# Value tiles with rows of 80 elements in place of 65 in a block-sparse attention and gated-MLP kernel

## The chip, the core and the metric

The kernel runs on one core of one Trainium2 chip. The metric is the device time of one execution in microseconds (us). The engines are TensorE (PE for its matrix products, PEld for its weight loads), VectorE (DVE), ScalarE (ACT), GpSimd (POOL) and the DMA queues, here nearly all issued by SyncE (SP).

## What is computed

Four batches of eight heads, 768 positions, 64 features for each head. A block-sparse mask (blocks of 32: neighbours, first and last, and three sampled blocks for each row of blocks) is applied to the scores; the softmax of them weights the value rows. The heads' outputs, side by side, are the input of a gated MLP whose second half is normalized and mixed over positions.

```python
scores = np.where(mask, scale * (q @ k.T), -1e9)
attn = exp(scores - max) / sum
x = (attn @ v) for each head, heads side by side      # 768 x 512 per batch
h = relu(x @ w_in); u, v = h[..., :512], h[..., 512:]
v_s = w_spatial @ ((v - mean) / sqrt(var + 1e-6)) + b_spatial
out = (u * v_s) @ w_out
```

## The kernel before

The 768 positions of a head are six chunks of 128 (NCH = 6). Heads are taken in pairs; there are 16 pairs (NP), four to a batch. For each head the kernel forms transposed scores chunk by chunk (keys on the partitions, queries along the row; L415 and L428), takes their exponential on ACT into `a_all` (L420 and L431), and multiplies with the values (L458 and L476). Masking rides in the score product as extra rows of `kq`.

**The value tiles.** There are six buffers `vv0` to `vv5` (line 85), used in turn by the pairs. Each holds, on each partition, 2 heads x 6 chunks x VA elements of bf16, with VA = 65: 64 features and a 1.0 written once at the start by POOL (L171). With the ones column the attention product also gives the softmax's denominator. A row of 65 elements has 130 bytes, and the rows lie one behind the other, so row (h, ci) begins 780 h + 130 ci bytes behind the tile's start. A tile takes 1,560 bytes of a partition, and the tiles start 1,568 bytes apart, each on a multiple of 32 bytes. Values are loaded as fp32 (`st_v`) and cast into `vv` by POOL (the helper `cast`, L137).

**The attention products.** One product takes a 128x128 block of `a_all` as the weights and one row of `vv` (128 partitions x 65) as the moving operand, and accumulates six chunks into 65 columns of a PSUM tile `ps_av`. The first batch, pairs 0 to 3, is worked in units, and `av_unit` (L458) issues eight products at a time, 36 times, 288 in all. The other twelve pairs go through `av_full` (L476), which issues the six products of one block of queries, 144 times, 864 in all. I call such a row of six or eight products a run.

**The order of the work** is written out by hand as slots. A slot issues the score products of one block, one run of attention products from some slots earlier, and, dealt out evenly, steps of the MLP of the batch before (L561, L630), so that PE has other matrix products between the runs. Scores go through two PSUM buffers (`sc`), so PE may be at most two slots ahead of ACT. After the last slot (178 us) only the last batch's MLP is left. Nothing in the order depends on the shape of `vv`.

Of the kernel before, what the change touches and what calls it, by code (L numbers as in the profile page):

```python
# [11 lines left out]
BF16 = mybir.dt.bfloat16  # L12
# [14 lines left out]
def kernel(  # L27
# [22 lines left out]
    NCH = S // 128  # L50
# [9 lines left out]
    VA = D + 1  # L60
# [9 lines left out]
    const = ctx.enter_context(tc.tile_pool(name="const", bufs=1))  # L70
# [11 lines left out]

    kq = const.tile([128, H, 2 * S], BF16, name="kq")
    NVV = 6
    vv = [const.tile([128, 2, NCH, VA], BF16, name=f"vv{s}") for s in range(NVV)]
    MR = slice(D, KR)
    MX = slice(D, 128)
    K_, Q_ = slice(0, S), slice(S, 2 * S)
# [344 lines left out]
    def av_tile(key, n):  # L433
        ps = psum.tile([128, 512], FP32, tag="av", bufs=2, name="ps_av")
        av_ref[key] = ps[:, 0:n * VA].rearrange("p (c d) -> p c d", d=VA)
        x_ref[key] = ps[:, 512 - TW // 2:512].bitcast(BF16)

    def normalize(ps, out, n):
        rc = work.tile([128, NCH, 1], FP32, tag="rc", bufs=2)
        nc.vector.reciprocal(out=rc[:, 0:n], in_=ps[:, :, D:VA])  # L440
        nc.vector.tensor_tensor(out=out, in0=ps[:, :, 0:D],  # L441
                                in1=rc[:, 0:n].to_broadcast([128, n, D]), op=ALU.mult)

    def av_unit(u, e):
        t, p = UNITS[u]
        if e == 0:
            av_tile(u, 2 * TC)
        for i in range(8 * e, 8 * e + 8):
            g, ci = divmod(i, NCH)
            if t == "h":  # L450
                h, qc, to, n = p, g, g, 2 * TC
                pp = 0
            else:
                (h, qc), n, pp = divmod(g, TC), TC, p
                to = qc * 2 + h
            at = (h * NCH + ci) * n * 128 if t != "h" else ci * n * 128
            at += qc * 128
            nc.tensor.matmul(out=av_ref[u][:, to, :], lhsT=a_ref[u][:, at:at + 128],  # L458
                             rhs=vv[pp % NVV][:, h, ci, :],
                             start=(ci == 0), stop=(ci == NCH - 1))  # L460
        if e == 2:
            a_ref.pop(u)
            if t == "h":
                if p == 0:
                    xn_ref[0] = work.tile([128, 2 * TC, 2, D], BF16, tag="xn0", bufs=1, name="xn0")
                normalize(av_ref.pop(u), xn_ref[0][:, :, p, :], 2 * TC)
            else:
                xn_ref[u] = work.tile([128, TC, 2, D], BF16, tag="xn3", bufs=3, name="xn3")
                normalize(av_ref.pop(u), xn_ref[u].rearrange("p c h d -> p (c h) d"), 2 * TC)

    def av_full(j, qc):
        p, h = divmod(j, 2)
        if qc == 0:
            av_tile(j, NCH)
        for ci in range(NCH):
            nc.tensor.matmul(out=av_ref[j][:, qc, :],  # L476
                             lhsT=a_ref["h", j][:, ci, qc * 128:(qc + 1) * 128],
                             rhs=vv[p % NVV][:, h, ci, :],
                             start=(ci == 0), stop=(ci == NCH - 1))
        if qc == NCH - 1:  # L480
            a_ref.pop(("h", j))
            if h == 0:
                xn_ref["p", p] = work.tile([128, NCH, 2, D], BF16, tag="xn", bufs=2, name="xn")
            normalize(av_ref.pop(j), xn_ref["p", p][:, :, h, :], NCH)
# [361 lines left out]
    for s in range(NS + LAG + 2):  # L846
        if s < S0:
            qk_unit(*divmod(s, 3))
        elif s < NS:
            j, ci = divmod(s - S0, NCH)  # L850
            qk_full(j + H, ci)
        early = at.get(s, [])
        for f in pre.get(s, []):
            f()
        for u, e in av_at.get(s, []):
            av_unit(u, e)
        if 0 <= s - LAG - S0 and s - LAG < NS:
            j, qc = divmod(s - LAG - S0, NCH)
            av_full(j + H, qc)
        for f in early:  # L860
            f()
        run_queue()
        for f in late.get(s, []):
            f()
        while post:
            post.pop(0)()
# [31 lines left out]
```

## Time and profile before

| | |
|---|---|
| three runs | 209.82, 210.37, 211.2 us; median 210.37 us |
| profiled execution, first to last instruction | span 208.3 us |
| PE busy | 201.0 us (97%), 2203 products recorded |
| ACT busy | 168.4 us (81%) |
| DVE busy | 146.8 us (70%) |
| POOL busy | 89.4 us (43%) |

The page gives the profiled execution by its span; the median run is 2.1 us longer than that span, and what lies around the span is taken to be these 2.1 us. Busy time of PE is the union of the products' durations; products overlap (one of 65 columns lasts 194 ns and the next starts long before it ends), so a full PE row doesn't say how fast PE goes. What a product costs in a stream is the time from its start to the next one's start, which the chain of waits shows.

### The profile page before, as it was taken

The numbers are of one execution on the slowest core, as the hardware profiler recorded it, in microseconds if no ns is written. First come the engines' busy times: TensorE is split into PE (matmuls) and PEld (weight loads), VectorE is DVE, ScalarE is ACT, GpSimd is POOL, SyncE is SP. The second block draws the span as 40 slices with busy tenths as digits, with TensorE's granted clock in tenths as the row PEclk, the third lists the DMA queues.
The fourth block names the chain that finished last, engine by engine and source line by source line (L and its number), as shares of the span: only waits on it lengthen the run. The fifth ranks groups of instructions, "written<-read, shape, count | busy, mean of one in ns | idle before, by whom it ended". The sixth has DMA issues, their size and how long they took to land.

```text
span 208.3 us, 5489 instructions
## 1 busy us (share of the span) xinstructions
PE 201.0 (97%) x2203; PEld 138.0 (66%) x2225; DVE 146.8 (70%) x315; ACT 168.4 (81%) x222; POOL 89.4 (43%) x186
## 2 busy tenths in 40 slices
PE   6899999999999999999999999999999999999993
PEld 6599888777766776667556676667665567445551
DVE  6888776989876766575975585456875666576871
ACT  6899999999999999989899878889899884266021
POOL 6888989767927964006757600006210000013000
PEclk9999999999999999999999999999999999999999
DMA  5999899999999999499987920499402010610016
GB/s 143 338 362 357 275 383 270 206 247 389 253 253 308 259 300 208 139 199 386 292 176 206 139 41 0 164 189 335 75 0 41 0 37 4 250 57 0 0 70 232
DMA packets 53053, 39.48 MB, mean 190 GB/s; under 512 B 33956, under 2 KB 47652, under 8 KB 53028
## 3 DMA queue, kind: packets, MB, share of 16 engines
q1 hardware_dynamic: 52596, 38.74, 70.0%
q10 hardware_dynamic: 432, 0.39, 0.6%
q8 instruction: 17, 0.28, 0.5%
q14 instruction: 8, 0.07, 0.1%
HBM read 24.77 MB, written 6.29 MB: 149 GB/s over the span
## 4 chain that ended last, share of the span: by engine, by line
PE 87%; DVE 4%; ACT 4%; DMA 2%; issue 1%; POOL 0%; ACTq 0%
PE ps L428 21%; PE ps_moe L630 17%; PE ps_moe L561 13%; PE ps_av L476 12%; PE ps L415 7%; PE ps_av L458 4%; PE ps_t L561 4%; PE ps_t L630 4%; PE ps_sc L630 2%; ACT a_all L420 2%; DVE stats L594 2%; DVE vn L185 2%; DMA st_q<-in_q_dram 2%; PE ps_sc L561 1%; PE ps L263 1%
## 5 line engine op out<-in xcount | busy, mean ns | idle before, releaser
L431 ACT ACTIVATE a_all<-ps 128x768 bf16<-128x768 f32 x144 | 113.4, 812 | 13.8 <-PE ps L428 6.2
L428 PE MATMUL ps<-kq 128*128 128x512 bf16 (+1 forms) x288 | 70.3, 326 | 0.3
L476 PEld LDWEIGHTS <-a_all 128*128 128x128 bf16 x864 | 46.6, 98 | 19.0
L476 PE MATMUL ps_av<-vv,a_all 128*128 128x65 bf16 x864 | 51.1, 194 | 0.1
L428 PEld LDWEIGHTS <-kq 128*128 128x128 bf16 x288 | 27.9, 97 | 23.6
L137 POOL CAST nat<-st_k 128x256 bf16<-128x256 f32 (+3 forms) x37 | 17.7, 509 | 38.7 <-DMA st_k<-in_k_dram 38.7
L420 ACT ACTIVATE a_all<-ps 128x1024 bf16<-128x1024 f32 x35 | 33.5, 1027 | 0.3
L630 PE MATMUL ps_moe<-w_spt,vn 128*128 128x512 bf16 (+1 forms) x144 | 33.1, 325 | 0.0
L598 POOL TENSOR_SCALAR std<-mv 128x3 f32<-128x3 f32 (+1 forms) x9 | 3.4, 376 | 48.7 <-DVE mv L595 48.5
L661 DVE TENSOR_TENSOR sb<-ps_moe,b_row 128x512 f32<-128x512 f32 x18 | 12.4, 690 | 14.5 <-PE ps_moe L630 14.2
L630 PE MATMUL ps_moe<-xt,w_in_t 128*128 128x256 bf16 (+1 forms) x108 | 21.7, 299 | 0.2
L415 PE MATMUL ps<-kq 128*128 128x256 bf16 x135 | 20.8, 275 | 0.8 <-DVE kq L211 0.6
L561 PE MATMUL ps_moe<-w_in_t,xt 128*128 128x512 bf16 x65 | 20.2, 378 | 0.2
L137 POOL CAST vv<-st_v 128x256 bf16<-128x256 f32 (+2 forms) x37 | 18.5, 533 | 3.9 <-DMA st_v<-in_v_dram 3.8
L137 POOL CAST nat<-st_q 128x256 bf16<-128x256 f32 (+2 forms) x41 | 19.2, 496 | 1.6 <-DMA st_q<-in_q_dram 1.5
L561 PE MATMUL ps_moe<-w_out_t,un 128*128 128x512 bf16 x64 | 19.4, 378 | 0.2
L441 DVE TENSOR_TENSOR xn<-ps_av,rc 128x384 bf16<-128x384 f32 (+1 forms) x36 | 18.5, 513 | 1.4 <-DVE rc L440 0.2
L664 DVE TENSOR_TENSOR un<-sb,un 128x512 bf16<-128x512 f32 x24 | 17.4, 727 | 1.5
L630 PEld LDWEIGHTS <-vn 128*128 128x128 bf16 x192 | 15.5, 97 | 4.4
L594 DVE BATCH_NORM_STATS2 stats<-vn 128x6 f32<-128x512 bf16 x24 | 16.5, 688 | 1.5 <-ACT vn L589 0.9
L211 DVE COPY osb<-ps_moe 128x512 f32<-128x512 f32 x12 | 8.3, 689 | 11.2 <-PE ps_moe L561 9.3
L211 DVE COPY kq<-tt 64x1536 bf16<-64x1536 bf16 x24 | 15.4, 641 | 0.6 <-DMA tt<-nat 0.2
(94 smaller groups left out, 241.6 us busy)
## 6 DMA issues: line engine op xcount, KB each, us to landing
out_dram<-osb SPq DMA_DIRECT2D x23, 256.0 KB, 2.1
st_k<-in_k_dram SPq DMA_DIRECT2D x15, 384.0 KB, 4.6
st_v<-in_v_dram SPq DMA_DIRECT2D x15, 384.0 KB, 6.2
st_q<-in_q_dram SPq DMA_DIRECT2D x12, 384.0 KB, 4.9
ws_f<-in_moe_w_spatial_dram SPq DMA_DIRECT2D x6, 384.0 KB, 5.5
w_f<-in_moe_w_in_dram SPq DMA_DIRECT2D x8, 256.0 KB, 6.3
w_f<-in_moe_w_out_dram SPq DMA_DIRECT2D x4, 256.0 KB, 5.4
st_q<-in_q_dram SPq DMA_DIRECT2D x3, 256.0 KB, 6.9
```

Of the source, the lines that this page charges most:

```text
L137: eng.tensor_copy(out=dst, in_=src)
L211: nc.vector.tensor_copy(out=o, in_=i)
L415: nc.tensor.matmul(out=ps[:, at:at + n * TW], lhsT=kq[:, h, ci * 128:(ci + 1) * 128], rhs=kq[:, h, qcols(t0, n)], start=True, stop=True)
L420: nc.scalar.activation(out=out, in_=ps, func=AF.Exp, scale=0.125)
L428: nc.tensor.matmul(out=ps[:, n0:n1], lhsT=kq[:, j % H, ci * 128:(ci + 1) * 128], rhs=kq[:, j % H, S + n0:S + n1], start=True, stop=True)
L431: nc.scalar.activation(out=a_ref["h", j][:, ci, :], in_=ps[:, 0:S], func=AF.Exp, scale=0.125)
L441: nc.vector.tensor_tensor(out=out, in0=ps[:, :, 0:D], in1=rc[:, 0:n].to_broadcast([128, n, D]), op=ALU.mult)
L476: nc.tensor.matmul(out=av_ref[j][:, qc, :], lhsT=a_ref["h", j][:, ci, qc * 128:(qc + 1) * 128], rhs=vv[p % NVV][:, h, ci, :], start=(ci == ...
L561: nc.tensor.matmul(out=ref["ps"][:, 0:w], lhsT=lhs(i), rhs=rhs(i), start=(i == 0), stop=(i == n - 1))
L594: nc.vector.bn_stats(out=stats, in_=self.vn[:, tcc, :])
L630: nc.tensor.matmul(out=o.rearrange("p (c t) -> p c t", c=n), lhsT=lhs(i)[:, (d0 + x) * 128:(d0 + x + 1) * 128], rhs=rhs(i), start=(i == 0) ...
L664: nc.vector.tensor_tensor(out=self.in_place(*area), in0=sb, in1=self.in_place(*area), op=ALU.mult)
```

## The change

The rows of a value tile become 80 elements (160 bytes) long, and the products read the first 65 of them. Row (h, ci) then begins 960 h + 160 ci bytes behind the tile's start, and the tiles are 1,920 bytes apart. Everything that is allocated behind the six tiles lies 2,112 bytes further on. The casts and the memset of the ones write the same elements at the new step. The instructions of every engine and their order are the same as before.

```diff
     NVV = 6
-    vv = [const.tile([128, 2, NCH, VA], BF16, name=f"vv{s}") for s in range(NVV)]
+    VS = 80
+    vv = [const.tile([128, 2, NCH, VS], BF16, name=f"vv{s}") for s in range(NVV)]
...
             nc.tensor.matmul(out=av_ref[u][:, to, :], lhsT=a_ref[u][:, at:at + 128],
-                             rhs=vv[pp % NVV][:, h, ci, :],
+                             rhs=vv[pp % NVV][:, h, ci, 0:VA],
                              start=(ci == 0), stop=(ci == NCH - 1))
...
                              lhsT=a_ref["h", j][:, ci, qc * 128:(qc + 1) * 128],
-                             rhs=vv[p % NVV][:, h, ci, :],
+                             rhs=vv[p % NVV][:, h, ci, 0:VA],
                              start=(ci == 0), stop=(ci == NCH - 1))
```

## Prediction

> **What bounds the kernel now.** I read the cores first, then who waits, then stretches of the span, then the chain. One core, full clock; and PE, once started, hardly waits for anyone:
>
> ```profile
> core 0: 208.3 us, clock 1.000
> PE wps L179 <- DVE tiny L157: 1.0, 1, 1.0
> PE psq L276 <- POOL nat L137: 0.6, 1, 0.6
> PE ps L415 <- DVE kq L211: 0.6, 1, 0.6
> ```
>
> These three are all of PE's own waits (us in total, times, longest). The stretches, with each engine's busy time:
>
> ```profile
> 11.00:43.00 32.00, 31.83 (x495) 28.01 (x498) 25.67 (x65) 31.52 (x34) 27.40 (x44) 1.00 1.07 309
> 43.00:178.00 135.00, 134.20 (x1484) 89.13 (x1497) 93.59 (x182) 117.88 (x158) 51.02 (x111) 1.00 0.72 177
> 178.00:208.00 30.00, 26.50 (x151) 14.31 (x150) 19.00 (x39) 10.23 (x18) 2.30 (x4) 1.00 0.26 97
> ```
>
> After the stretch's length the columns are PE, PEld, DVE, ACT, POOL. From 43 to 178 us PE is full and ACT has 17 of 135 us free: PE sets the pace there. From 11 to 43 us (the first batch, L458) PE and ACT are both full, ACT with 32.00 - 31.52 = 0.48 us free. So a nanosecond taken off a product's step comes off the time in the second stretch, and only within ACT's 0.48 us in the first.
>
> **What one attention product costs.** The chain of waits gives streams of products with no wait in them (start, length, then engine, tile, line, count):
>
> ```profile
> 14.64 0.45 PE ps L263 x8
> 183.88 1.73 PE ps_t L561 x8
> 187.34 0.87 PE ps_t L630 x8
> 11.60 0.51 PE ps_av L458 x16
> 49.53 0.19 PE ps_av L476 x6
> ```
>
> The first three are products of 128, 512 and 256 columns, each with its own weight load: 0.45/8 = 56 ns, 1.73/8 = 216 ns and 0.87/8 = 109 ns. Per column that is (216 - 56)/384 = 0.417 ns. Down from 128 columns to 65 it leaves 56.3 - 63 x 0.417 = 30.0 ns, down from 256 it leaves 108.8 - 191 x 0.417 = 29.1 ns; with 10 ns of rounding on each piece the two agree between 29.4 and 29.8. I take 29.6 ns as the step of a 65-column product that nothing disturbs. The attention products take 0.51/16 = 31.9 ns (L458) and 0.19/6 = 32 ns (L476). The finer number for L476 comes from its group:
>
> ```profile
> L476 PE MATMUL ps_av<-vv,a_all 128*128 128x65 bf16 x864 | 51.1, 194 | 0.1
> L458 PE MATMUL ps_av<-vv,a_all 128*128 128x65 bf16 x288 | 14.7, 194 | 0.0
> L476 PEld LDWEIGHTS <-a_all 128*128 128x128 bf16 x864 | 46.6, 98 | 19.0
> ```
>
> 51.1 us over 144 runs is 354.9 ns a run; less one duration of 194 ns, five steps remain: 32.2 ns each. So each attention product is 32.2 - 29.6 = 2.6 ns slower than its columns ask. Is the row's place the cause? The trace holds a test. In head 0 the rows of a run begin 0, 2, 4, 6, 8, 10 bytes past a multiple of 16; in head 1 they begin 12, 14, 0, 2, 4, 6 past one. A row that doesn't begin on a multiple of 16 shares its first 16 bytes with the end of the row that was read just before, unless it is the first of its run. So a run of head 0 has five rows that share and a run of head 1 has four. L476 alone, the twelve stretches with head 0 (first, last, sum) and the twelve with head 1:
>
> ```profile
> 46.20:50.68 4.48, 2.13 (x36) 1.00 1.03 354
> ...
> 168.86:173.91 5.05, 2.13 (x36) 1.00 0.21 42
> sum 59.56, PE 25.57; mean PE 2.13
> ```
>
> ```profile
> 51.03:55.52 4.49, 2.12 (x36) 1.00 1.21 253
> ...
> 174.15:178.08 3.93, 2.12 (x36) 1.00 0.18 67
> sum 60.77, PE 25.48; mean PE 2.12
> ```
>
> Each sum holds 72 runs of six. Head 1 is (25.57 - 25.48)/72 = 1.25 ns shorter a run, with one sharing row fewer. The place of a row does count, and an aligned row is the quicker one.
>
> **The change, part by part.**
>
> *The reads.* All twelve rows of a tile now begin on a multiple of 32 bytes, and none shares its first 16 bytes with the row before. The lower end is to let each sharing row that goes give what the one in head 1 gives: 4.5 rows a run x 1.25 ns x 144 runs = 0.81 us, and about 5.5 rows x 1.25 ns x 36 runs = 0.25 us in L458: 1.06 us. The upper end is that all 1,152 products fall to the lowest step above, 29.4 ns: 864 x 2.8 + 288 x 2.5 = 3.1 us. I take a point near the upper end, because in today's runs every aligned row is followed by a sharing one, which may wait for what the aligned row did not; a single replacement then shows only part, while after the change no such follower is left. With the undisturbed step of 29.6 ns: L476 gives 864 x 2.6 ns = 2.25 us, all of it in the stretch where PE alone sets the pace. L458 gives 288 x (31.9 - 29.6) = 0.66 us, of which ACT's free 0.48 us lets 0.48 us through. Sum: 2.25 + 0.48 = 2.73 us.
>
> *A rule that speaks against this.* The Trainium skill's page "SBUF — State Buffer" (Specifications (TRN2)) gives SBUF 16-byte lines, says that a line needs at least two hits for full bandwidth and that each crossing to a new line costs. A row of 130 bytes touches nine such lines at any even start, so by counting lines nothing changes; and the new layout leaves one lone element in the ninth line of every row, which by the two-hits rule is a cost that before only rows on a multiple of 16 had. The two sums above disagree with that second half: head 1, which has more such rows, is the quicker. No row here separates the crossing cost itself.
>
> *The writes.* POOL casts the same elements with a step of 160 bytes in place of 130:
>
> ```profile
> L137 POOL CAST vv<-st_v 128x256 bf16<-128x256 f32 x30 | 12.7, 460 | 2.7 <-DMA st_v<-in_v_dram 2.6
> L137 POOL CAST nat<-st_k 128x256 bf16<-128x256 f32 x30 | 12.8, 464 | 38.4 <-DMA st_k<-in_k_dram 38.4
> L171 POOL MEMSET vv<- 128x12 bf16 x6 | 0.4, 180 | 0.0
> ```
>
> Into `nat`, whose rows of 64 lie on multiples of 128 bytes, the same cast takes 464 ns against 460 into today's rows, so alignment is worth between -4 and +4 ns a cast; over 30 casts that is 0.1 us of POOL time either way, and PE's list has no wait for `vv` at all. I take 0. What hides it is POOL's free time (51 of 135 us busy). The six memsets write 12 lone elements, each in a place of its own before and after: 0, with at most their 0.4 us either way on a POOL queue that runs ahead of the first casts.
>
> *The shift* of the later tiles by 2,112 bytes keeps their places to a multiple of 64 bytes. No row shows such a shift; between the heads above, a different place inside a tile moved a run by 1.25 of 355 ns, and that for rows that changed against 16 bytes, so I bound it at 0.4% of PE's time on other lines, 0.5 us either way, and take 0.
>
> **The sum.** The profiled span of 208.3 us less 2.73 us is 205.6 us; with the 2.1 us that lie between the span and the median run, 207.6 us, or 1.3% under 210.37.
>
> **The rivals.**
>
> *Part only.* The aligned row's gain really is 1.25 ns and doesn't grow when its neighbours are aligned too, or the weight loads (98 ns each, six of them overlapping in a run) hold the pair of load and product near 31 ns. For it: the only measured replacement gave that little. Against: streams of other widths with the same loads stand on the straight line of columns. Time: 210.4 - 1.1 = 209.3 us.
>
> *No effect: the change doesn't do what it says.* The step of 32.2 ns is set by the weight load or by the odd number of columns, and the heads differ for another reason (their place in the slots). For it: loads and products come in pairs in every run. Against: 0.09 us between the heads over 72 runs, in sums that differ in the same direction in nearly each pair. Time: 210.4 us.
>
> *Slower.* Place: the read of a row of `vv` in L458 and L476. Today a row that shares its first 16 bytes gets them from what was just read; afterwards each row must open its ninth line for one element alone. Price: a line holds eight columns, 8 x 0.417 = 3.3 ns, on the 648 + 198 rows that share today: 2.8 us, so 213.2 us. It decides as soon as a fresh line costs more than the sharing does, that is if aligned runs are longer than 355 ns. Against it: head 1 has one fresh row more and is shorter. The skill's two-hits rule in "SBUF — State Buffer" would point this way.
>
> **How the numbers follow.** My forecast (nearly the whole excess goes, 207.0 to 208.4 us): 0.57. Part only (208.4 to 209.8): 0.22. No effect: 0.15. Slower: 0.06. The predicted time is that of the first, 207.6 us. The range reaches from the upper end of the read's gain with a little for the shift and the spread of runs, 210.4 - 3.1 - 0.4 = 206.9, up over the second case to 210.0; left out are the slower case and most of the third, about 0.2. Since cases of no gain are few, no second range is needed. Faster by over 1% (about what a measurement of this kernel can tell from no change) means under 208.27 us: nearly all of the first case, 0.54. Within 1%: the rest of it, part only and no effect, 0.40. Slower by over 1%: 0.06.
>
> **What would show it.** In the profile after: a run of L476 in the chain takes 0.18 us in place of 0.19; the group of L476 falls from 51.1 to 144 x (194 + 5 x 29.6) ns = 49.2 us; the sums of the two heads become equal, near 24.6 us each; the durations of a product stay at 194 ns and the casts at 460; in the first batch ACT stays full, and PE may show a small wait for it; from 43 to 178 us the stretch shrinks by about 2.2 us with PE still full. The forecast is wrong if the run of L476 stays above 350 ns (no effect or part only), or if it falls and a new wait on PE stands beside it, which would mean that another engine was closer behind than ACT's 17 us say.

## Result and the profile after

The changed kernel takes 208.44 us (median of 6 runs, 208.17 to 208.81) against 210.38 us before (6 runs, 209.82 to 211.57): a ratio of 0.991 with a 95% interval of [0.988, 0.993]. Measured once more on one chip beside another layout (below) the ratio was 0.992 [0.991, 0.994]. The change is a gain of 1.6 to 1.9 us, 0.8 to 0.9%. The forecast had the direction and the cause right and the time inside its range; its size of 2.7 us is too large.

The profiled execution's span fell from 208.3 to 206.6 us. PE's own waits after the change (us in total, times, longest; there were three before), and the first two stretches with the busy time of PE, PEld, DVE, ACT and POOL:

```profile
PE wps L180 <- DVE tiny L158: 1.0, 1, 1.0
PE ps L416 <- DVE kq L212: 0.6, 1, 0.6
```

```profile
11.00:43.00 32.00, 31.84 (x499) 27.89 (x501) 25.26 (x67) 31.41 (x35) 27.41 (x44) 1.00 1.06 301
43.00:178.00 135.00, 134.17 (x1486) 87.90 (x1499) 94.24 (x183) 117.78 (x158) 49.68 (x110) 1.00 0.75 182
```

Nothing new stands in PE's way: no wait for ACT in the first batch, none for POOL or DMA later, and PE is still full. So no part of the expected gain was lost to another engine. In the chain of waits a run of L477 now takes 0.18 us in place of 0.19. What is smaller is the gain at its source. The groups of the attention products (line numbers are one higher than before):

```profile
L477 PE MATMUL ps_av<-vv,a_all 128*128 128x65 bf16 x864 | 49.7, 193 | 0.1
L459 PE MATMUL ps_av<-vv,a_all 128*128 128x65 bf16 x288 | 14.3, 193 | 0.0
```

The full products' group fell from 51.1 to 49.7 us, where 49.2 was forecast. By the same working, 49.7 us over 144 runs less one duration leaves (345.1 - 193)/5 = 30.4 ns a step: it was 32.2, and 29.6 was forecast. The two sums by head, which differed by 0.09 us before, now differ by 0.02 (head 0, then head 1; the first of the twelve stretches and the sum):

```profile
45.58:50.01 4.43, 2.07 (x36) 1.00 1.17 303
sum 59.09, PE 24.84; mean PE 2.07
```

```profile
50.36:54.80 4.44, 2.07 (x36) 1.00 1.14 315
sum 60.22, PE 24.82; mean PE 2.07
```

That is the sign by which the forecast wanted to know the mechanism: with every row free of sharing, it no longer matters which head a run belongs to. How much of it reaches the end is read from the first and last start of each line's products, before and then after (durations, then "first to last"):

```profile
L476 PE MATMUL ps_av<-vv,a_all x864: 192/193/198, 46.2 to 177.9; 128*128 128x65 bf16 x173
L458 PE MATMUL ps_av<-vv,a_all x288: 190/194/198, 10.5 to 42.6; 128*128 128x65 bf16 x144
```

```profile
L477 PE MATMUL ps_av<-vv,a_all x864: 191/193/198, 45.6 to 176.3; 128*128 128x65 bf16 x173
L459 PE MATMUL ps_av<-vv,a_all x288: 191/193/197, 10.2 to 42.0; 128*128 128x65 bf16 x144
```

The stretch of the full products is 131.7 us long before and 130.7 after: 1.0 us. The stretch of the units went from 32.1 to 31.8: 0.3 us. The remaining 0.4 of the span's 1.7 us is 0.3 us before the first attention product, which started at 10.2 in place of 10.5 us, and 0.1 us behind the last one. The reads alone don't bring that earlier start: three profiles below of layouts without sharing start at 10.8 or 10.9 us. But both profiles of the changed kernel start early (10.2 and 10.1), so whether this layout has a part in it stays open.

But five steps of each run gave 1.4 us, and the stretch around them shrank by only 1.0. The difference is in the groups that follow the runs on PE. The MLP's products before, and after:

```profile
L630 PE MATMUL ps_moe<-w_spt,vn 128*128 128x512 bf16 (+1 forms) x144 | 33.1, 325 | 0.0
L630 PE MATMUL ps_moe<-xt,w_in_t 128*128 128x256 bf16 (+1 forms) x108 | 21.7, 299 | 0.2
L561 PE MATMUL ps_moe<-w_in_t,xt 128*128 128x512 bf16 x65 | 20.2, 378 | 0.2
L561 PE MATMUL ps_moe<-w_out_t,un 128*128 128x512 bf16 x64 | 19.4, 378 | 0.2
```

```profile
L631 PE MATMUL ps_moe<-w_spt,vn 128*128 128x512 bf16 (+1 forms) x144 | 33.3, 326 | 0.0
L631 PE MATMUL ps_moe<-xt,w_in_t 128*128 128x256 bf16 (+1 forms) x108 | 21.8, 300 | 0.2
L562 PE MATMUL ps_moe<-w_in_t,xt 128*128 128x512 bf16 x65 | 20.3, 379 | 0.2
L562 PE MATMUL ps_moe<-w_out_t,un 128*128 128x512 bf16 x64 | 19.5, 379 | 0.2
```

None of these was touched, and each grew by 0.1 or 0.2 us, 0.5 us together. The start times of single products in the traces, to a nanosecond, show where (the views above round them). From the first start of a run to the start of the product behind it, the 144 runs took 1.5 us less in all. The first product behind a run then took longer to the next start: 220 in place of 215 ns with 512 columns and 113 in place of 108 ns with 256 (L630), 0.6 us in all over both MLP lines. The products that follow it kept their steps to within 0.4 ns, together 0.1 us less. So 1.5 - 0.6 + 0.1 = 1.0 us is left, which is the stretch. Part of what a run saves by its start times is still owed when the run is over, and the product behind it pays. Net of that a product of a run became (131.7 - 130.7) us / 864 = 1.2 ns quicker, which from 32.2 ns leaves about 31 ns.

### The profile page after: what moved, and what is told of

Same layout as the page of the kernel before. It is cut to its first block, busy times and chain, and to the rows that moved or that the text cites. A ratio compares the mean times of both kernels' runs of the same rounds, so it can differ in the third digit from the quotient of the medians.

```text
span 206.6 us, 5489 instructions
## 1 busy us (share of the span) xinstructions
PE 200.1 (97%) x2203; PEld 136.7 (66%) x2225; DVE 145.9 (71%) x315; ACT 167.8 (81%) x222; POOL 87.8 (43%) x186
## 4 chain that ended last, share of the span: by engine, by line
PE 88%; ACT 5%; DVE 4%; issue 1%; ACTq 0%
PE ps L429 21%; PE ps_moe L631 17%; PE ps_moe L562 13%; PE ps_av L477 11%; PE ps L416 7%; PE ps_av L459 4%; PE ps_t L562 4%; PE ps_t L631 4%; PE ps_sc L631 3%; ACT a_all L421 2%; DVE stats L595 2%; DVE vn L186 2%; PE wps L180 2%; PE ps_sc L562 1%; PE ps L264 1%
## 5 line engine op out<-in xcount | busy, mean ns | idle before, releaser
L477 PEld LDWEIGHTS <-a_all 128*128 128x128 bf16 x864 | 45.6, 97 | 19.0
L477 PE MATMUL ps_av<-vv,a_all 128*128 128x65 bf16 x864 | 49.7, 193 | 0.1
L631 PE MATMUL ps_moe<-w_spt,vn 128*128 128x512 bf16 (+1 forms) x144 | 33.3, 326 | 0.0
L599 POOL TENSOR_SCALAR std<-mv 128x3 f32<-128x3 f32 (+1 forms) x9 | 2.9, 317 | 46.7 <-DVE mv L596 46.5
L138 POOL CAST vv<-st_v 128x256 bf16<-128x256 f32 (+2 forms) x37 | 16.9, 487 | 3.6 <-DMA st_v<-in_v_dram 2.6
L186 DVE TENSOR_SCALAR vn<-ps_moe 128x512 bf16<-128x512 f32 x18 | 12.4, 687 | 4.0 <-PE ps_moe L562 3.6
```

The lines of the kernel that those rows point to most:

```text
L138: eng.tensor_copy(out=dst, in_=src)
L186: nc.vector.tensor_scalar(out=out, in0=in0, scalar1=s1, scalar2=s2, op0=o0, **kw)
L477: nc.tensor.matmul(out=av_ref[j][:, qc, :], lhsT=a_ref["h", j][:, ci, qc * 128:(qc + 1) * 128], rhs=vv[p % NVV][:, h, ci, 0:VA], start=(ci ...
L631: nc.tensor.matmul(out=o.rearrange("p (c t) -> p c t", c=n), lhsT=lhs(i)[:, (d0 + x) * 128:(d0 + x + 1) * 128], rhs=rhs(i), start=(i == 0) ...
```

## Experiments

Three questions: is it the alignment of a row, or that it begins in the 16 bytes where the row just read ended; does anything else in the change count; and why is the aligned step 30.4 and not 29.6 ns?

**Rows 146 bytes apart.**

```diff
-    VS = 80
+    VS = 73
```

> Rows 146 bytes apart: most of them begin off a multiple of 16, but 17 bytes lie between the end of a row and the start of the next, so none begins in the 16 bytes that the row before it ended in. If the sharing of 16 bytes with the row just read is what cost time, the group of the full attention product falls to the 49.7 us of the changed kernel and the time to about 208.4 us (ratio 0.991). If it is alignment, rows off a multiple of 16 stay slow: 51.1 us, and a ratio of 1.00.

```profile
L477 PE MATMUL ps_av<-vv,a_all 128*128 128x65 bf16 x864 | 49.8, 193 | 0.0
```

Ratio 0.993 [0.991, 0.995]; the full products' stretch is 46.3 to 176.7, 130.4 us. Rows that begin off a multiple of 16, and of 4, are as quick as rows on a multiple of 32 (16 bytes lie between two rows here, not the 17 of the expectation; they share nothing either way). It is not the alignment. The time, 208.73 us, is 0.3 us above the expected 208.4; the last experiment comes back to it.

**Rows 144 bytes apart.**

```diff
-    VS = 80
+    VS = 72
```

> Rows 144 bytes apart: each begins on a multiple of 16, every second one off a multiple of 32. Sharing of 16 bytes: as the changed kernel, 49.7 us for the group and a ratio of 0.991. If units of 32 bytes count (by alignment or by sharing), half the rows stay slow: about 50.4 us and a ratio near 0.995.

```profile
L477 PE MATMUL ps_av<-vv,a_all 128*128 128x65 bf16 x864 | 49.6, 193 | 0.0
```

Ratio 0.993 [0.990, 0.995], stretch 130.5 us. Half the rows lie off a multiple of 32, and some begin in the 32 bytes where the row before ended; nothing is lost by either. So units of 32 bytes don't count. Units of 8 don't fit the kernel before: the fifth row of a run of head 0 begins 8 bytes past a multiple of 16 and shares no 8 bytes with the row before it, yet by the start times in the trace its step is 32.4 ns, as long as the two before it (32.5 ns each). The unit that counts is 16 bytes.

**The layout of before, read backwards.**

```diff
-        for ci in range(NCH):
+        for ci in reversed(range(NCH)):
...
-                             start=(ci == 0), stop=(ci == NCH - 1))
+                             start=(ci == NCH - 1), stop=(ci == 0))
```

> The kernel before, tiles with 65 elements, but the full attention products take the six chunks from the last to the first, so that a row never begins in the 16 bytes that the product just before ended in; the places of all rows are those of before. Sharing with the row just read: the group falls to 49.7 us, the units' products stay as before at 14.7 us, and the time falls by about 1.5 us (ratio 0.993). Alignment: nothing changes, 51.1 us and 1.00.

```profile
L476 PE MATMUL ps_av<-vv,a_all 128*128 128x65 bf16 x864 | 49.8, 194 | 0.0
L458 PE MATMUL ps_av<-vv,a_all 128*128 128x65 bf16 x288 | 14.7, 194 | 0.0
L476 PE MATMUL ps_av<-vv,a_all x864: 191/193/199, 46.2 to 176.6; 128*128 128x65 bf16 x173
```

Ratio 0.995 [0.993, 0.996], stretch 130.4 us. The median is 1.25 us lower, where about 1.5 was expected, and the stretch 1.3 us shorter. Every byte lies where it lay before, and the full products have the whole gain; the units, whose order stayed, have none. So the cost belongs to which row is read just before, not to a row's place.

**Aligned rows that share.**

```diff
-    vv = [const.tile([128, 2, NCH, VA], BF16, name=f"vv{s}") for s in range(NVV)]
+    vt = [const.tile([128, 2 * NCH * D + 16], BF16, name=f"vv{s}") for s in range(NVV)]
...
+        at = (h * NCH + ci) * D
+        return vt[s][:, at:at + VA]
```

> Rows 128 bytes apart of which 65 elements are read: every row begins on a multiple of 32 bytes, and the last element read is the first of the next row, so five of the six rows of a run begin in the 16 bytes that the row before ended in. The 65th column then holds sums of values in place of the softmax's denominator: that sum is left out. Sharing: the group stays at 51.1 to 51.3 us although all rows are aligned. Alignment: it falls to 49.7 us.

```profile
L481 PE MATMUL ps_av<-vv,a_all 128*128 128x65 bf16 x864 | 51.1, 194 | 0.1
```

The opposite corner: every row on a multiple of 128 bytes, each beginning in the 16 bytes in which the row before ended, and the group is that of the kernel before to the digit (a single run took 210.23 us beside 209.94). Of what was put forward, the four together leave only the sharing.

**The shift alone.**

```diff
+    const.tile([128, 1056], BF16, name="gap")
```

> The kernel before with an unused tile behind the six value tiles, which moves all that lies behind by the 2,112 bytes of the change and leaves the value tiles alone. Both theories on the reads: 51.1 us for the group and a ratio of 1.00 (within 0.3%). If part of the change's gain is the shift of the later tiles, the ratio is below 0.997.

Ratio 1.000 [0.998, 1.001], the group at 51.0 us. The later tiles' places are worth nothing that shows, within 0.2%.

**One column less.**

```diff
-                             rhs=vv[p % NVV][:, h, ci, 0:VA],
+                             rhs=vv[p % NVV][:, h, ci, 0:D],
```

> The changed kernel, with products over 64 columns in place of 65; the ones column is not read, so the softmax's denominator is left out (the division takes another column). In the changed kernel a step is 29.2 ns except for about every fifth, which is 35 ns. If that longer step comes from the ninth 16-byte piece that a row of 65 needs for one element, it goes and the six products of a run take 6 x 28.9 = 173 ns to the next product, 181 before: the group near 48.4 us. If it comes from the pairs of weight load and product as such, the mean step stays at 30.2 ns and the group falls only by the last product's 0.4 ns a run, to 49.6 us.

```profile
L477 PE MATMUL ps_av<-vv,a_all 128*128 128x64 bf16 x864 | 49.0, 194 | 0.1
```

49.0 us lies between the two numbers (a single run took 207.39 us). The step is (340.3 - 194)/5 = 29.3 ns, 1.1 ns less than with 65 columns, where one column is worth 0.4 ns. By the group alone that only leans to the ninth piece. The start times tell more: with 65 columns one step of a run, that of its second product, lasts 34.3 ns on average and the other four 29.1 to 29.8; with 64 columns none of the five averages over 29.6. So the long step goes with the ninth piece. The group stays above 48.4 us because the steps that are left are 29.5 ns and not 28.9. The next two put it to the test at another place.

**72 and 73 columns.**

```diff
-    VS = 80
+    VS, VC = 80, 72      # then 73
...
-                             rhs=vv[p % NVV][:, h, ci, 0:VA],
+                             rhs=vv[p % NVV][:, h, ci, 0:VC],
```

> The changed kernel with products over 72 columns: 144 bytes, nine full 16-byte pieces (the seven columns more are ones that nothing reads). By the columns alone a step is 29.2 + 7 x 0.417 = 32.1 ns. If a product is paced by the larger of its columns and of its 16-byte pieces at 8 x 0.417 = 3.3 ns each (nine: 30.0 ns), columns win here, no long step is left, and the group of the full product is 144 x (197 + 5 x 32.1) ns = 51.5 us. If every fifth step is long for another reason that comes with the pairs of load and product, the mean step is 33.1 ns and the group 52.2 us.

> As the kernel with 72 columns, with one column more, which alone lies in a tenth 16-byte piece. Pacing by pieces: ten x 3.3 = 33.3 ns a step, and the group is 144 x (197 + 5 x 33.4) ns = 52.4 us, 0.9 us over the one with 72 columns. By columns alone: 32.5 ns and 51.8 us, 0.3 us over it.

The groups with 72 and then with 73 columns:

```profile
L477 PE MATMUL ps_av<-vv,a_all 128*128 128x72 bf16 x864 | 51.6, 197 | 0.0
```

```profile
L477 PE MATMUL ps_av<-vv,a_all 128*128 128x73 bf16 x864 | 52.6, 196 | 0.0
```

Forecast by pieces 51.5 and 52.4, measured 51.6 and 52.6 (single runs took 211.11 and 212.29 us): steps of (358.3 - 197)/5 = 32.3 and (365.3 - 196)/5 = 33.9 ns. Seven columns from 65 to 72 cost 1.9 ns, the one column from 72 to 73 costs 1.6, and the one from 64 to 65 cost 1.1. The steps one by one, from the start times in the traces (mean ns from a start to the next, first to fifth product of a run of six):

| columns | 1st | 2nd | 3rd | 4th | 5th |
|---|---|---|---|---|---|
| 64 | 28.3 | 29.5 | 29.6 | 29.6 | 29.5 |
| 65 | 29.2 | 34.3 | 29.8 | 29.1 | 29.1 |
| 72 | 31.7 | 31.7 | 31.6 | 32.5 | 32.5 |
| 73 | 32.5 | 37.7 | 33.0 | 32.6 | 32.5 |

The two widths whose last column lies alone in a 16-byte piece have a long second step, and the two that fill their pieces have none. The mean steps fit a simple rule: a product is paced by its columns, at 0.417 ns each and some 2 ns more (29.2 ns for 65), or by its pieces at 3.3 ns each, whichever takes longer. It gives 28.8, 30.0, 32.1 and 33.3 ns, and 29.3, 30.4, 32.3 and 33.9 were measured. Why the pieces' time comes as one long step is not shown.

**The changed kernel again, beside 146 bytes.**

> The changed kernel again. By the stretches of its profile the reads are worth 1.3 us (1.0 us in the full products, 0.3 us in the units), a ratio of 0.994; its first measurement gave 0.991 with an interval that ends at 0.993. If the reads are all there is, the ratio here lies between 0.992 and 0.995; if there is a second gain of some 0.6 us outside the products, it stays at 0.991.

> Rows 146 bytes apart again, beside the changed kernel on one chip. If only the sharing of 16 bytes counts, the two have the same time within 0.2%; if the 32-byte places add something, the changed kernel is the faster one by 0.3% or more.

The full products and the units of the changed kernel, then the full products with 146 bytes:

```profile
L477 PE MATMUL ps_av<-vv,a_all x864: 191/193/198, 45.7 to 176.3; 128*128 128x65 bf16 x173
L459 PE MATMUL ps_av<-vv,a_all x288: 190/193/198, 10.1 to 42.1; 128*128 128x65 bf16 x144
L477 PE MATMUL ps_av<-vv,a_all x864: 191/193/198, 46.2 to 176.6; 128*128 128x65 bf16 x173
```

Ratios 0.992 [0.991, 0.994] and 0.993 [0.992, 0.994], 208.53 and 208.72 us. The changed kernel falls where the reads alone would put it, though its interval doesn't exclude a small gain besides. 146 bytes is the same within the spread, and no layout here beats the changed one. The six profiles with 65 columns and no sharing in the full products have stretches of 130.4 to 130.7 us, the three with sharing of 131.6 to 131.8: the reads of the full products are worth 1.0 to 1.3 us. The units' part is less steady: here their stretch is 32.0 us, against 31.8 in the first profile of the same kernel and 32.1 before.

## Why the prediction came out as it did

- *PE sets the pace from 11 us on:* right. Whatever came off the stretch of the runs came off the span, and no new wait appeared.
- *The cause is a row that begins in the 16 bytes where the row just read ended:* right, though read from two sums that differ by 0.4%. The prediction spoke of sharing and of alignment as one thing; rows of 146 bytes, the reversed order and the overlapping aligned rows each tell them apart, and it is the sharing.
- *The undisturbed step of 29.6 ns, on all 1,152 products:* this term was mis-sized. It was drawn as a straight line down from products of 128, 256 and 512 columns, all of them a whole number of 16-byte pieces. A row of 65 elements has a ninth piece for its last one. At 3.3 ns a piece, nine give 30.0 ns; the changed kernel's step is 30.4. L476 was forecast at 2.25 us and gave 1.0 us: its runs gave 1.5 us up to the start of the product behind them, and that product took 0.6 us back. L458 was forecast at 0.48 us and gave 0.3 us; the sum was forecast at 2.73 us and is 1.3 us in the stretches, beside a measured difference of 1.6 to 1.9 us between medians.
- *Why the point near the upper end:* the reason was that a row which follows an aligned one may wait for what that one did not, and that after the change no such follower is left. The first half is what happens. By the start times of the trace before, the five steps of a run are 29.3, 35.0, 32.5, 32.5 and 32.4 ns in head 0 and 29.2, 35.0, 29.1, 33.8 and 32.6 in head 1. The third row of head 1, which doesn't share, is 3.4 ns quicker than that of head 0, and the next is 1.3 ns slower. The second half is wrong: a follower is left, the MLP's product behind each run, which takes up to 5 ns more. The two heads' runs differ by 1.9 ns in their start times; the sums of busy time, which hold the last product's duration too, showed 1.25. With 1.9 ns the working of the lower end gives 1.6 us in place of 1.06. The forecast (207.6) and the rival "part only" (209.3) were equally near: 208.44 lies midway, and by the prediction's own bounds just inside "part only", which began at 208.4.
- *The rule that was weighed:* the Trainium skill's page "SBUF — State Buffer" (Specifications (TRN2)) says that each crossing to a new 16-byte line costs. The prediction noted that the count of lines stays at nine and that no row separated the cost. The runs do: from 64 to 65 and from 72 to 73 columns the step rises by 1.1 and 1.6 ns where a column is worth 0.4. With the line count pacing the step (9 x 3.3 = 30.0 ns), the sum would have been 864 x 2.2 + 288 x 1.9 = 2.4 us, still before what the product behind a run takes back. Its two-hits rule does not make sharing the better choice: lone elements in the ninth line cost less than sharing did. The prediction's own argument against that rule was weaker than it looked: of rows on a multiple of 16 each head has one, and head 1 has more lone elements only if the row 14 bytes past a multiple is counted, whose lone element lies in its first line and is shared.
- *Writes, memsets, shift:* 0, right. The shift alone has a ratio of 1.000. The casts into `vv` were 425 ns after and 460 before, but 468 ns in the layout of 144 bytes and 475 with the old rows and the shift. So they spread by far more than the 4 ns that were allowed; whether the layout moves them is not shown, and they are off the path.
- *The rivals of the other side:* a fresh line for each row doesn't cost more than sharing; in the overlapping layout sharing came back and the group with it.

## What to carry to other kernels

When short products follow one another on PE, let no moving operand begin in the 16 bytes where the one before ended: here 1.1 to 1.5 ns of pace for each product, for a few bytes of padding (7 elements do as well as 15) or for a change of order at no cost in memory. Price a short product by its 16-byte pieces as well as by its columns before extending a straight line from long ones. And where a replacement already stands in the trace of before, measure it by start times, together with the product behind it: a step that gets shorter can make the next one longer.

## What was not expected of the hardware

- Sharing 16 bytes with the previous read makes a product slower, not quicker: 32.2 against 30.4 ns a step.
- One column that lies alone in a new 16-byte piece costs more than a column: the mean step is 29.3 ns for 64 columns, 30.4 for 65, 32.3 for 72 and 33.9 for 73.
- A quicker run hands part of its time to the untouched product behind it: 5 ns in the changed kernel (215 to 220 ns, and 108 to 113), 0.6 us of 1.5 us saved up to there. With rows 146 bytes apart, and with the order reversed, the same products of 512 columns take only about 1.5 ns more. Which part of PE holds that debt, and why the layouts differ in it, stays open; no run here looked into it.
